# A spectral filter and a gated convolution on one core: forward part by 32 channels, back half in time order, a list that knows PSUM and transfers

## The chip, the cores and the metric

The kernel runs on 1 core of one Trainium2 chip. The metric is device microseconds of one launch. The kernel before was run three times: 344.11, 345.82 and 351.01 us, median 345.82.

The engines are named as in the profile: PE (TensorE, with its weight loads as PEld), DVE (VectorE), ACT (ScalarE), POOL (GpSimd) and SP (SyncE). SP only issues transfers here, and POOL mostly.

## The reference

The input x has 8 images (batch) of 3200 points by 256 channels. Every channel is filtered in the frequency domain over the 3200 points; the result goes through a gated unit with a causal convolution of five taps.

```
X = rfft(x, axis=1)                         # 1601 frequencies
y = irfft(X * (filt_r + 1j*filt_i), n=3200) # y: (8, 3200, 256)

gate = sigmoid(sum_k conv_w[k] * y_padded[:, k:k+3200, :])   # k = 0..4, four zeros ahead
val  = y @ w_val                                             # 256 x 256
out  = (gate * val) @ w_out                                  # 256 x 256, float32
```

## The kernel before, in words

The 3200 points are 100 x 32: point n = 32a + r. The transform is done in two steps of matmuls, and so is its inverse; between the two steps of the inverse the data goes through a scratch tensor in HBM (`escr`).

Per image, in the order of the data:

- `load_x`: eight loads on POOL's queue, each four values of r, all a and all channels, cast to bf16 (tile `xt`, ten buffers).
- `s1` (L417): first transform, two matmuls of 512 columns per load. `so` copies its PSUM to `so` on ACT or DVE, in an interleaved layout of four channels. `turn` (L436): four transposes of 32x32 blocks on DVE, which take pairs of bf16 as float32.
- `s2` (L446): second transform, seven units of two (the last of one) frequency groups. `xs` copies it to bf16, `zed` (L464) multiplies with the real filter (`za`) and, in a second instruction, with the imaginary one (`zb`), both on DVE.
- `inva` (L477): first step of the inverse. `ue` copies, `wr` (L498) writes the unit to `escr` through SP's queue.
- `lv` (L508, L509): eight reads of four values of r, two transfers each, only after all seven writes. `ib` (L518): second step of the inverse, `ye` (L528, ACT) copies it to `yt`, ordered by r, then a. `halo` (L535, L537) copies the last four r, shifted by one a, ahead of the first on POOL.
- Eight blocks of four r by 100 a: `conv` (L545) with diagonal weights, `gate` (L554, sigmoid on ACT), `val` (L563), `gv` (L573, the gate product on DVE), `outp` (L583), `oe` (copy `o<-ps`), `store` (L597, L598, two transfers on SP's queue).

L408 is the copy on ACT and L410 the copy on DVE, both called from `so`, `xs`, `ue`, `oe` and the tables. All PSUM tiles are of one kind, 128 x 1024 float32 with four buffers. The first 20 us also make the tables of the transforms (`cf_t`, `w_t`, `a_t`, `b_t`, `ci_t`) and load the filters (`fr_t`, `fi_t`), whose upper half of rows is a copy made by SP (L253, "doubling").

The order on every engine is written by `Plan`: a list of tasks, each with an engine and a cost in us, a rank, what it depends on, which buffers it takes and gives back, and a time until its transfer has landed (`land`). It is played once at build time: at each moment the ready task with the lowest rank gets the free engine. The resulting order is fixed; on the chip each engine runs its own in order and waits for what is not there. Transfers are only a delay in this list, and PSUM only a count of four:

```
add(f"wr{b},{u}", {"SP": 0.45}, r + 1, ..., lambda e, b=b, u=u: wr(b, u), take=..., land=3.0)
add(f"lv{b},{i}", {"SP": 0.8}, r - 2, [f"wd{b},{u}" for u in range(len(UCH))], ..., land=3.0, give=())
add("fl0", {"none": 0.0}, -100, [], None, land=26.0)
add("fl1", {"none": 0.0}, -100, [], None, land=34.0)
```

## Time and profile before

| what | value |
|---|---|
| median of three runs | 345.82 us (344.11 to 351.01) |
| profiled execution, first to last instruction | 344.8 us |
| busy: PE, ACT, DVE, POOL | 288.3, 267.8, 256.4, 68.0 us |
| mean granted TensorE clock | 0.970 |
| moved by DMA | 70.91 MB, mean 206 GB/s |
| first transform of image 0 starts | 6.0 us |
| first convolution starts | 79.1 us |
| last matmul of `outp` starts | 338.6 us |

The span is one execution; the median is of other executions of the same kernel and lies 1.0 us above it. Busy time is the time in which at least one instruction of the engine ran. A group's line in the profile gives its line in the code, the engine, the operation, what it writes and reads, the count, the busy time, the mean in ns of one, and the idle time of the engine ahead of it with what ended it.

### The profile page before, as it was taken

The numbers are of one execution on the slowest core, as the hardware profiler recorded it, in microseconds if no ns is written. First come the engines' busy times: TensorE is split into PE (matmuls) and PEld (weight loads), VectorE is DVE, ScalarE is ACT, GpSimd is POOL, SyncE is SP. The second block draws the span as 40 slices with busy tenths as digits, with TensorE's granted clock in tenths as the row PEclk, the third lists the DMA queues.
The fourth block names the chain that finished last, engine by engine and source line by source line (L and its number), as shares of the span: only waits on it lengthen the run. The fifth ranks groups of instructions, "written<-read, shape, count | busy, mean of one in ns | idle before, by whom it ended". The sixth has DMA issues, their size and how long they took to land.

```text
span 344.8 us, 9785 instructions
## 1 busy us (share of the span) xinstructions
PE 288.3 (84%) x3988; PEld 191.6 (56%) x3988; DVE 256.4 (74%) x340; ACT 267.8 (78%) x309; POOL 68.0 (20%) x142
## 2 busy tenths in 40 slices
PE   2634677639999987999779997999999999999992
PEld 0023031326667755776457764776577677766762
DVE  4985477938698996889849994989798999734541
ACT  3954286928898987898849986998999789887663
POOL 8687455210112112110211011100100000001000
PEclk9999999969999999899989998999999999999997
DMA  6999999995899989898869969795677568778544
GB/s 95 155 168 163 213 192 195 206 238 168 199 232 247 272 233 231 245 229 251 170 200 207 271 176 250 214 245 171 199 208 221 156 204 261 234 214 248 160 144 143
DMA packets 57421, 70.91 MB, mean 206 GB/s; under 512 B 8608, under 2 KB 37152, under 8 KB 57376
## 3 DMA queue, kind: packets, MB, share of 16 engines
q1 hardware_dynamic: 45344, 55.20, 53.4%
q0 software_dynamic: 12032, 15.08, 29.0%
q8 instruction: 31, 0.51, 0.6%
q14 instruction: 14, 0.11, 0.1%
HBM read 43.78 MB, written 39.85 MB: 243 GB/s over the span
## 4 chain that ended last, share of the span: by engine, by line
PE 43%; DMA 24%; DVE 15%; ACT 7%; issue 4%; POOL 4%; SPq 1%; ACTq 0%; POOLq 0%; DVEq 0%
DMA vt<-escr 13%; PE ps L583 12%; PE ps L545 10%; DMA xt<-in_x_dram 6%; PE ps L563 6%; DVE tt L436 5%; DVE gv L573 5%; PE ps L417 5%; PE ps L518 5%; PE ps L477 4%; DMA fi_t<-in_filt_i_dram 3%; PE ps L446 3%; ACT o L408 2%; DVE xs L410 2%; POOL xt L161 2%
## 5 line engine op out<-in xcount | busy, mean ns | idle before, releaser
L573 DVE TENSOR_TENSOR gv<-ps,gt 128x800 bf16<-128x800 f32 x64 | 62.7, 980 | 19.9 <-PE ps L563 13.6
L408 ACT ACTIVATE o<-ps 100x1024 f32<-100x1024 f32 x59 | 61.0, 1035 | 16.9 <-PE ps L583 12.9
L410 DVE CAST xs<-ps 128x1024 bf16<-128x1024 f32 (+1 forms) x44 | 50.4, 1145 | 29.0 <-PE ps L446 29.0
L583 PE MATMUL ps<-wo_t,gv 128*100 128x256 bf16 x512 | 68.7, 278 | 2.7 <-DVE gv L573 1.1
L545 PE MATMUL ps<-yt,dg_t 64*64 64x400 bf16 x1280 | 67.3, 339 | 0.3
L408 ACT ACTIVATE so<-ps 128x1024 bf16<-128x1024 f32 x53 | 54.5, 1029 | 15.9 <-PE ps L417 11.1
L528 ACT ACTIVATE yt<-ps 128x800 bf16<-128x800 f32 x64 | 53.9, 846 | 15.9 <-PE ps L518 15.7
L583 PEld LDWEIGHTS <-gv 128*100 128x100 bf16 x512 | 54.5, 125 | 18.6 <-DVE gv L573 9.0
L161 POOL DMA_DIRECT2D xt<-in_x_dram x64 | 35.4, 556 | 124.5 <-PE ps L417 119.8
L554 ACT ACTIVATE gt<-ps 128x800 bf16<-128x800 f32 x64 | 54.1, 847 | 6.5 <-PE ps L545 5.3
L417 PE MATMUL ps<-xt,cf_t 100*128 100x512 bf16 x128 | 47.5, 462 | 12.2 <-DMA xt<-in_x_dram 11.2
L563 PE MATMUL ps<-yt,wv_t 128*128 128x400 bf16 x256 | 54.4, 335 | 0.5 <-ACT gt L554 0.5
L408 ACT ACTIVATE u<-ps 128x1024 bf16<-128x1024 f32 (+1 forms) x46 | 44.9, 982 | 7.2 <-PE ps L477 6.6
L518 PE MATMUL ps<-ci_t,vt 104*128 104x100 f16 x512 | 34.3, 212 | 16.5 <-DMA vt<-escr 16.4
L518 PEld LDWEIGHTS <-vt 104*128 104x128 bf16 x512 | 29.6, 100 | 30.1 <-DMA vt<-escr 19.8
L545 PEld LDWEIGHTS <-dg_t 64*64 64x64 bf16 x1280 | 34.5, 108 | 17.3 <-issue 4.2
L436 DVE STREAM_TRANSPOSE tt<-so 128x1024 f32<-128x1024 f32 x32 | 40.6, 1272 | 3.2 <-ACT so L408 3.2
L464 DVE TENSOR_TENSOR za<-xs,fr_t 128x1024 bf16<-128x1024 bf16 (+1 forms) x56 | 36.1, 649 | 1.4 <-ACT xs L408 0.2
L464 DVE TENSOR_TENSOR zb<-xs,fi_t 128x1024 bf16<-128x1024 bf16 (+1 forms) x56 | 35.5, 640 | 1.4 <-DMA fi_t<-in_filt_i_dram 1.4
L477 PE MATMUL ps<-zb,b_t 64*64 64x256 bf16 x416 | 29.7, 294 | 4.4 <-DVE zb L464 4.4
L477 PE MATMUL ps<-za,a_t 64*64 64x256 bf16 x416 | 30.3, 298 | 2.4 <-DVE za L464 2.1
L446 PE MATMUL ps<-tt,w_t 64*64 64x256 bf16 x416 | 24.2, 305 | 9.0 <-DVE tt L436 4.4
(93 smaller groups left out, 181.9 us busy)
## 6 DMA issues: line engine op xcount, KB each, us to landing
out_dram<-o SPq DMA_DIRECT2D x64, 384.0 KB
xt<-in_x_dram POOLq DMA_DIRECT2D x64, 200.0 KB, 6.7
escr<-u SPq DMA_DIRECT2D x48, 256.0 KB
vt<-escr SPq DMA_DIRECT2D x64, 192.0 KB
escr<-u SPq DMA_DIRECT2D x8, 128.0 KB
vt<-escr SPq DMA_DIRECT2D x64, 16.0 KB
out_dram<-o SPq DMA_DIRECT2D x64, 16.0 KB
fr_t<-in_filt_r_dram POOLq DMA_DIRECT2D x8, 56.0 KB, 4.7
```

Source lines behind the costliest of these rows:

```text
L408: nc.scalar.activation(dst, src, AF.Copy, **kw)
L410: nc.vector.tensor_copy(dst, src)
L417: nc.tensor.matmul(ps[:, 512 * h:512 * h + 512], lhsT=cf_t[0:L].rearrange("p h c i -> p (h c i)"), rhs=xv[:, DQ // 2 * h:DQ // 2 * h + DQ ...
L436: nc.vector.transpose(dst, src)
L464: (nc.vector if e == "DVE" else nc.gpsimd).tensor_tensor(z[:, :, 0:nm * D], xs_[:, :, 0:nm * D], f[:, :, m0:m0 + nm, :].rearrange("p h m d ...
L477: nc.tensor.matmul(ps[64 * h:64 * h + 64, 512 * t + D * a:512 * t + D * a + D], lhsT=tab[rows, h, m0 + a, :], rhs=zz[w][rows, h, D * a:D * ...
L518: nc.tensor.matmul(ps[:, o:o + L], lhsT=v[0:NV, a, 128 * dh:128 * dh + 128], rhs=ci_t[0:NV, :], start=True, stop=True)
L545: nc.tensor.matmul(ps[64 * dh:64 * dh + 64, 512 * r:512 * r + RC * L], lhsT=dg_t[rows, dh, k, :], rhs=y[rows, dh, RC * j + k:RC * j + k + ...
L554: nc.scalar.activation(g[...], ps[:, :].rearrange("p (h n) -> p h n", h=2)[:, :, 0:RC * L], AF.Sigmoid)
L563: nc.tensor.matmul(ps[:, 512 * eh:512 * eh + RC * L], lhsT=wv_t[:, dh, 128 * eh:128 * eh + 128], rhs=y[:, dh, H + RC * j:H + RC * j + RC, ...
L573: nc.vector.tensor_tensor(gv_[...], ps[:, :].rearrange("p (h n) -> p h n", h=2)[:, :, 0:RC * L], g[...], op=ALU.mult)
L583: nc.tensor.matmul(ps[0:L, D * a:D * a + D], lhsT=gv_[:, eh, L * a:L * a + L], rhs=wo_t[:, eh, :], start=(eh == 0), stop=(eh == 1))
```

## The change

- **Loads.** Four loads of eight r per image instead of eight of four; six `xt` buffers instead of ten. All four are held until the last `s1` of the image.
- **Forward part by 32 channels.** `s1` makes one chunk of 32 channels over all r with four matmuls of 256 columns, so it needs the whole image of x. There are eight chunks; each is copied and then transposed by itself (eight transposes of 512 pairs), in a plain layout without interleaving.
- **Filter products.** Real and imaginary filter lie in one tile `f_t`; one DVE instruction makes both products, reading `xs` twice.
- **Inverse.** Reads and `ib` go in seven pieces of five or four r. `ye` may run on ACT or DVE and writes y in time order; the scale moves into the tables. y has two fixed tiles with four zero points ahead; the halo copies go.
- **Back half by up to 512 points in time order.** Blocks of 4, 4, 4, 4, 3, 3, 3 groups of 128 points. `conv` reads y shifted by k points and needs all of the image's y. `gv` writes its result so that `outp` has 128 output rows per matmul pair; an image has 25 such pairs of matmuls instead of 32. `store` is one transfer per block.
- **The list.** PSUM tiles are named by the list (four tags, the one that came free first); transfers are a resource `DMA` with a cost; ranks come from a table of offset and step per kind of task; costs and landing times are others.

```diff
-RC = 4
-NCH = R // RC
+NQ = 8
+CQ = 32
+NX = 4
-ICH = [NCH - 1] + list(range(NCH - 1))
+ICH = [(0, 5), (5, 5), (10, 5), (15, 5), (20, 4), (24, 4), (28, 4)]
+BLK = [(0, 4), (4, 4), (8, 4), (12, 4), (16, 3), (19, 3), (22, 3)]
...
+PAR = dict(
+    PERIOD=72.97,
+    OFF=dict(cv=156.07, ia=-128.75, ib=-197.48, lv=-31.3, lx=-117.23, op=28.61, s1=-95.0, s2=19.16, vl=14.51,
+             z=-219.82),
+    STEP=dict(cv=10.032, ia=33.214, ib=0.337, lv=2.627, lx=23.302, op=46.79, s1=0.678, s2=9.262, vl=9.77,
+             z=39.345),
+)
+NPS = 4
+def rank_of(par, s, b, k):
+    return par["PERIOD"] * b + par["OFF"][s] + par["STEP"][s] * k
...
+            slot = None
+            if "ps" in t["take"]:
+                slots.sort()
+                held[n] = slot = slots.pop(0)[1]
...
+    NXT, NSO, NXS, NZ, NU, NVB, NGB, NOB = 6, 3, 3, 3, 4, 4, 3, 4
+    y_t = [cpool.tile([128, 2, H + N], BF16, name=f"y{n}") for n in range(2)]
...
     def psum():
-        return pp.tile([128, 1024], FP32, name="ps", tag="ps")
+        return pp.tile([128, 1024], FP32, name="ps", tag=f"ps{g['slot']}")
...
+        for j in range(NX):
+            nc.tensor.matmul(ps[:, w * CQ * j:w * CQ * j + w * CQ],
                              lhsT=cf_t[0:L].rearrange("p h c i -> p (h c i)"),
-                             rhs=xv[:, DQ // 2 * h:DQ // 2 * h + DQ // 2], start=True, stop=True)
+                             rhs=st["X", b, j][0:L, :, CQ * q:CQ * q + CQ],
+                             start=True, stop=True)
...
     def turn(b, q):
         if q == 0:
-            st["T", b] = tpool.tile([128, DQ, 32, E], BF16, name="tt")
-        w = DQ // 4
-        src, dst = (t_[:, w * q:w * q + w].rearrange("p q r e -> p (q r e)").bitcast(FP32)
-                    .rearrange("p (q r w) -> p q w r", r=32, w=E // 2)
-                    for t_ in (st["SO", b], st["T", b]))
-        nc.vector.transpose(dst, src)
+            st["T", b] = tpool.tile([128, 32, D], BF16, name="tt")
+        src = st.pop(("SO", b, q))[...].rearrange("p r w -> p (r w)").bitcast(FP32)
+        dst = st["T", b][...].rearrange("p i d -> p (i d)").bitcast(FP32)
+        V.transpose(dst.rearrange("p (i k) -> p k i", i=32)[:, CQ // 2 * q:CQ // 2 * q + CQ // 2],
+                    src.rearrange("p (r k) -> p k r", r=32))
...
+    def zed(b, u):
+        V.tensor_tensor(z[:, :, :, 0:nm * D],
+                        t[:, :, 0:nm * D].unsqueeze(1).to_broadcast((128, 2, 2, nm * D)),
+                        f_t[:, :, :, m0:m0 + nm, :].rearrange("p w h m d -> p w h (m d)"),
+                        op=ALU.mult)
...
     def ye(b, i, e):
+        copy(e, y_t[b % 2][:, :, H:H + N].rearrange("p h (n r) -> p h n r", r=R)
+             [:, :, :, r0:r0 + nr],
+             ps[:, :].rearrange("p (h n) -> p h n", h=2)[:, :, 0:nr * L]
+             .rearrange("p h (r n) -> p h n r", n=L))
-    def halo(b):
...
     def gv(b, j):
+        V.tensor_tensor(
+            t[:, :, 0:nm, :].rearrange("p h a n -> p h n a"),
+            ps[:, :].rearrange("p (h n) -> p h n", h=2)[:, :, 0:128 * nm]
+            .rearrange("p h (n a) -> p h n a", a=nm),
+            gt[:, :, 0:128 * nm].rearrange("p h (n a) -> p h n a", a=nm), op=ALU.mult)
     def outp(b, j):
-        for a in range(RC):
+        for a in range(nm):
             for eh in range(2):
+                nc.tensor.matmul(ps[:, D * a:D * a + D], lhsT=t[:, eh, a, :],
+                                 rhs=wo_t[:, eh, :], start=(eh == 0), stop=(eh == 1))
     def store(b, j):
-        nc.sync.dma_start(out=dst[0:96], in_=o[0:96])
-        nc.sync.dma_start(out=dst[96:L], in_=o[96:L])
+        dst = out[b, 128 * m0:128 * m0 + 128 * nm, :].rearrange("(p a) d -> p (a d)", a=nm)
+        nc.sync.dma_start(out=dst, in_=o[:, 0:nm * D])
...
+                add(f"li{b},{j}", {"POOL": 0.6}, r, ["pool"],
+                    lambda e, b=b, j=j: load_x(b, j), take=("xt",), land=1.0)
+                add(f"lx{b},{j}", {"DMA": 2.2}, r, [f"li{b},{j}"], None, land=2.0)
...
+            add(f"t{b},{q}", {"DVE": 0.68}, r, [f"so{b},{q}"] + ([f"t{b},{q - 1}"] if q else []),
+                lambda e, b=b, q=q: turn(b, q), take=("t",) if q == 0 else (), give=("so",))
...
+            add(f"wi{b},{u}", {"SP": 0.35}, r, [f"ue{b},{u}"] + ([f"wi{b},{u - 1}"] if u else []),
+                lambda e, b=b, u=u: wr(b, u), take=("e",) if u == 0 else (), land=0.6)
+            add(f"wd{b},{u}", {"DMA": 0.44 * nm}, r, [f"wi{b},{u}"], None, give=("u",), land=2.0)
...
+            add(f"vi{b},{i}", {"SP": 0.7}, r, [f"wd{b},{u}" for u in range(len(UCH))],
+                lambda e, b=b, i=i: lv(b, i), take=("v",), land=0.6)
+            add(f"lv{b},{i}", {"DMA": 0.14 * nr}, r, [f"vi{b},{i}"], None, land=1.6)
...
+    add("pool", {"none": 0.0}, -100, [], None, land=19.0)
+    for c, t in enumerate((22.0, 27.0)):
+        add(f"fl{c}", {"none": 0.0}, -100, [], None, land=t)
```

507 lines of the change are left out of this document (245 added, 262 removed).

## The prediction

> **What bounds the kernel now.** I read the page first, then three stretches side by side, then the chain in order of time, then the groups by form, and last the first 50 us instruction by instruction. The page:
>
> ```profile
> span 344.8 us, 9785 instructions
> ...
> PE 288.3 (84%) x3988; PEld 191.6 (56%) x3988; DVE 256.4 (74%) x340; ACT 267.8 (78%) x309; POOL 68.0 (20%) x142
> ...
> DMA vt<-escr 13%; PE ps L583 12%; PE ps L545 10%; DMA xt<-in_x_dram 6%; PE ps L563 6%; DVE tt L436 5%; DVE gv L573 5%; PE ps L417 5%; PE ps L518 5%; PE ps L477 4%; DMA fi_t<-in_filt_i_dram 3%; PE ps L446 3%; ACT o L408 2%; DVE xs L410 2%; POOL xt L161 2%
> ```
>
> No engine is full over the whole span, and the chain hops between PE and three transfers. The stretches (us, then busy us of PE, PEld, DVE, ACT, POOL, then clock, DMA share, GB/s) say why:
>
> ```profile
> 60.00:80.00 20.00, 11.20 (x187) 7.03 (x189) 12.66 (x17) 12.39 (x15) 3.80 (x8) 0.83 0.97 220
> 0.00:80.00 80.00, 45.21 (x459) 19.50 (x463) 53.93 (x111) 47.10 (x54) 43.54 (x91) 0.96 0.98 181
> 80.00:300.00 220.00, 204.99 (x3052) 145.32 (x3045) 185.26 (x213) 190.85 (x223) 23.45 (x49) 0.98 0.82 219
> 300.00:344.80 44.80, 38.10 (x488) 26.77 (x484) 17.25 (x17) 29.89 (x34) 0.97 (x2) 0.96 0.62 184
> ```
>
> The first 80 us are a start-up: PE is busy for 45.2 of them, DMA is at 0.98. From 80 to 300 PE has 205 of 220, ACT 191, DVE 185: all three are close together, PE ahead. At the end PE works nearly alone. The start-up ends where the causal convolution begins:
>
> ```profile
> L545 PE MATMUL ps<-yt,dg_t x1280: 327/329/539, 79.1 to 335.5; 64*64 64x400 bf16 x183
> ```
>
> Pieces of the chain (start, us, what):
>
> ```profile
> 34.36 11.60 DMA xt<-in_x_dram
> ...
> 63.07 11.63 DMA vt<-escr
> ...
> 91.92 5.78 DMA escr<-u
> ...
> 167.33 6.89 DMA vt<-escr
> ...
> 202.51 0.88 PE ps L583 x8
> ...
> 242.86 4.60 DMA vt<-escr
> ...
> 338.99 1.02 ACT o L408
> ```
>
> So PE's last matmul ends at 338.9. From 80 to there it has 288.3 - 45.2 = 243.1 us of work in 258.9 us, 0.939. The kernel is 80 us of start-up, then a stretch that PE fills, then 344.8 - 338.9 = 5.9 us of last copy and store. The median shown, 345.82, is 1.0 above the span; I add that 1.0 at the end.
>
> **The change part by part.** The groups by form:
>
> ```profile
> L583 PE MATMUL ps<-wo_t,gv 128*100 128x256 bf16 x512 | 68.7, 278 | 2.7 <-DVE gv L573 1.1 <-ACT yt L528 0.2
> L573 DVE TENSOR_TENSOR gv<-ps,gt 128x800 bf16<-128x800 f32 x64 | 62.7, 980 | 19.9 <-PE ps L563 13.6 <-ACT gt L554 6.1
> L408 ACT ACTIVATE o<-ps 100x1024 f32<-100x1024 f32 x59 | 61.0, 1035 | 16.9 <-PE ps L583 12.9 <-ACT yt L528 1.5 <-DMA vt<-escr 1.4
> L554 ACT ACTIVATE gt<-ps 128x800 bf16<-128x800 f32 x64 | 54.1, 847 | 6.5 <-PE ps L545 5.3
> L528 ACT ACTIVATE yt<-ps 128x800 bf16<-128x800 f32 x64 | 53.9, 846 | 15.9 <-PE ps L518 15.7
> L410 DVE CAST xs<-ps 128x1024 bf16<-128x1024 f32 x38 | 46.4, 1222 | 28.8 <-PE ps L446 28.8
> L408 ACT ACTIVATE u<-ps 128x1024 bf16<-128x1024 f32 x40 | 41.4, 1040 | 5.8 <-PE ps L477 5.1 <-ACT xs L408 0.4 <-DMA vt<-escr 0.2
> L436 DVE STREAM_TRANSPOSE tt<-so 128x1024 f32<-128x1024 f32 x32 | 40.6, 1272 | 3.2 <-ACT so L408 3.2
> L161 POOL DMA_DIRECT2D xt<-in_x_dram x64 | 35.4, 556 | 124.5 <-PE ps L417 119.8 <-DMA xt<-in_x_dram 2.1 <-DMA fi_t<-in_filt_i_dram 0.9
> L464 DVE TENSOR_TENSOR za<-xs,fr_t 128x1024 bf16<-128x1024 bf16 x48 | 32.8, 689 | 1.2
> L464 DVE TENSOR_TENSOR zb<-xs,fi_t 128x1024 bf16<-128x1024 bf16 x48 | 32.5, 682 | 1.4 <-DMA fi_t<-in_filt_i_dram 1.4
> L410 DVE CAST xs<-ps 128x512 bf16<-128x512 f32 x6 | 4.0, 659 | 0.2 <-PE ps L446 0.2
> L408 ACT ACTIVATE u<-ps 128x512 bf16<-128x512 f32 x6 | 3.6, 593 | 1.5 <-PE ps L477 1.5
> L464 DVE TENSOR_TENSOR za<-xs,fr_t 128x512 bf16<-128x512 bf16 x8 | 3.2, 405 | 0.2 <-ACT xs L408 0.2
> ```
>
> *PE.* Output points go in 25 groups of 128 per image in place of 32 of 100, so 50 matmuls of L583 replace 64. Eight back to back took 0.88 us, 0.11 each: 14 x 0.11 = 1.5 us per image, 12.3 us in all. PE is the fullest engine from 80 us on, so I count all of it. Convolution, value, first transform and inverse stream the same columns in other pieces: nothing.
>
> *ACT and DVE, per image.* ACT's slope is (1040 - 593)/512 = 0.87 ns per element, so 768 cost about 0.82 us. Output copies: 8 x 1.035 becomes 4 x 1.035 + 3 x 0.82, -1.7. Gate and inverse copies have the same elements in seven instructions, -0.2 each. Gate product: 8 x 0.98 becomes 4 x 1.22 + 3 x 0.95, -0.1. Filter products: slope (689 - 405)/512 = 0.555 ns, so 2048 elements take 1.26 against 1.37 for the pair, -0.8 over the image. Transposes: eight of half the size, 0.66 each by the ratio of the casts (659 to 1222), against four of 1.27, +0.4. Sum -2.5 of 65.5 us, some 10 us per engine over the run. These engines are not the bound; it can only shorten the 258.9 - 243.1 = 15.8 us in which PE stands idle after 80. Bounds 0 and 15.8; I take 4, nearer to nothing, because the waits on vt above (4.6 to 6.9 us) are part of it and stay.
>
> *Access steps, which no row shows.* The transposes read and write at steps of 8 bytes now; after the change they read at 64 and write at 512. The gate product writes single bf16 values 256 bytes apart. The inverse copy (L528) reads PSUM 400 bytes apart and writes runs of 10 bytes. A gain has no reason. The nearest rows are the plain forms above, so I take no extra; the other end is twice the rate per element. It is priced as a rival. The Trainium skill speaks against the change here: "SBUF — State Buffer", in the note on cachelines under "Door 1: The DMA port swizzle", says that SBUF wants at least two hits per 16-byte line and that each access to a new line is penalised. No run here shows it; a step of 8 bytes keeps that rule and the new steps break it.
>
> *The product with a repeated operand.* It could lose its 0.555 ns per element and go at the 1.1 ns of the casts; I take 0.555, since its inner runs stay contiguous bf16 like the rows'. The Trainium skill ("VectorE: DVE Perf Modes", "What auto-detection actually checks") asks only for 16-bit tensors with step one, which agrees.
>
> *Queues.* On POOL 32 of 64 loads (0.556 each) and the halo copies go; POOL waits most of the time, so nothing in the middle. On SP 28 issues per image replace 39; SP waits on ACT, nothing. A load's transfer is longer, but four bring the same image. The wait added is that the first transform needs all of x and the convolution all of y: behind these PE instructions stand the other image's matmuls, which the list has put where it believes the data to be there.
>
> *Start-up.* What sets it (start, us, engine, line, what it waited for):
>
> ```profile
> 20.89 3.32 SPq L253 DMA_DIRECT2D fi_t<-fi_t  x2
> ...
> 28.28 1.29 DVE L464 TENSOR_TENSOR zb<-xs,fi_t 128x1024 bf16<-128x1024 bf16 x2 [1.40 <-DMA fi_t<-in_filt_i_dram]
> ...
> 31.50 2.63 SPq L253 DMA_DIRECT2D fi_t<-fi_t  x2
> ...
> 42.85 1.28 DVE L464 TENSOR_TENSOR za<-xs,fr_t 128x1024 bf16<-128x1024 bf16 x2
> ...
> 46.00 1.03 PE L417 MATMUL ps<-xt,cf_t 100*128 100x512 bf16 x2 [0.42 <-DMA xt<-in_x_dram]
> ```
>
> The doubling of the first filter half was issued by 24.2 and used 4.1 later; the second, issued by 34.1, is thus in at about 38. The products that need it ran only at 42.85: DVE held copies of image 1 ahead of them, whose x came till 46. The new list has transfers as a resource and ranks most of image 0's products ahead of image 1. So: filters at 37 (four fewer loads ahead on POOL, -1), four products 42, inverse and copy 43.5, write 5.8 (the escr row above) -> 49.5, read 5.8 (between 4.6 and 6.9) -> 55, seven inverse chunks and copies of about 1 us -> 62. The convolution starts at 62 in place of 80. The list itself believes in filters at 27 and an idle POOL at 19, both too early by these rows, so it will still queue things behind unlanded data; the bounds are 55 and 80.
>
> *Sum.* PE work 288.3 - 12.3 = 276.0. By 60 PE had done 45.2 - 11.2 = 34.0, by 62 say 35. Left 241, at 0.939 takes 256.7. 62 + 256.7 + 5.9 = 324.6, less 4, is 320.6; with the 1.0, **321 us**, 7% less.
>
> **The rivals.** *The strides cost (slower).* Place: gate product, transposes, inverse copies. At twice the rate: 6400 x 1.10 ns = 7.0, 4096 x 1.10 = 4.5, 6400 x 0.87 = 5.6, together 17.1 us per image on DVE and ACT. They would need (524.2/8 - 2.5 + 17.1)/2 = 40 us each per image, against 276/8 = 34.5 for PE, and become the bound. At 0.92 of their time (they now reach 0.855 together in the middle) that is 43.5, against 34.5/0.939 = 36.7 for PE in my forecast: +6.8 over seven overlapped images, 321 + 48 = 369. At two fifths of that price, 19 us, nothing measurable is left of the gain; from two thirds on it is slower than before. For it: the old layout's 8-byte steps. Against: no row shows any loss. The skill's cacheline rule would bring this outcome.
>
> *The start-up stays* (the new list stalls behind its own optimistic landings; the change does not do what it says there). Convolution at 80: 276.0 - 45.2 = 230.8, over 0.939 = 245.8; 80 + 245.8 + 5.9 - 4 + 1 = 329. For: the landings above. Against: image 1 goes first in fewer places of the list.
>
> *The product falls to the slow rate.* 2048 x 1.1 + 0.1 = 2.35 against 1.37, +6.4 us per image on DVE, from 32 to 38, some 3 us per image beyond PE: about 345.
>
> *DMA becomes the bound.* At 0.82 over 220 us it needs 180 us of the middle; my forecast, 25 us shorter with 18 of them in the start-up, leaves some 210. It would not bind, but keeps the vt waits; inside my range.
>
> **How the numbers follow.** Forecast 321 (own range 309 to 331): 0.43. Start-up stays, 325 to 340: 0.15. A part of the stride price, 334 to 354: 0.13. The whole of it, 352 to 385: 0.24. Slow product: 0.05. The range of 302 to 360 reaches into the stride rival, because it holds much of the chance, and to the lower bound of start-up and idle time. About 2% (339 to 353 as no change) is what a measurement can tell here. Faster 0.57: the forecast, most of the second, a bit of the third; same 0.17; slower 0.26.
>
> **What would show it.** First convolution near 62; L583 at 400 matmuls and near 54 us busy; transposes near 0.66, gate products near 1.22 and 0.95, inverse copies near 1.02 us; the product near 1.26. If transposes, gate products and inverse copies show 1.4 times these, the strides decide and I am wrong. If the first convolution stands at 75 or later, the start-up step is wrong. If PE is busy under 0.9 after its start, the order in the queues is.

## The result, and the profile after

The changed kernel takes **516.07 us** (median; 514.44 to 519.21) against 345.44 for the kernel before on the same chip: **1.495 times as long, interval 1.485 to 1.505**. I had forecast 321, with a range of 302 to 360. The slower side stood there only as a rival (the strides cost, 369 us), and that was far too small as well.

The page of the changed kernel: span, then busy time and share of each engine.

```profile
span 512.7 us, 9126 instructions
...
PE 324.1 (63%) x3786; PEld 193.9 (38%) x3812; DVE 454.6 (89%) x326; ACT 250.3 (49%) x268; POOL 41.0 (8%) x88
```

Before, PE led with 84% and DVE had 74%. Now DVE has 454.6 us of work against 256.4, and PE is at 63%. In stretches (us, then busy us of PE, PEld, DVE, ACT, POOL, then clock, DMA share, GB/s), cut at the first convolution:

```profile
0.00:85.20 85.20, 39.99 (x510) 27.78 (x511) 62.70 (x111) 44.23 (x50) 31.12 (x70) 0.74 0.84 167
85.20:300.00 214.80, 146.08 (x1669) 84.35 (x1684) 202.74 (x123) 113.46 (x120) 9.83 (x18) 0.84 0.53 146
```

From 85 to 300 DVE is busy for 202.7 of 214.8 us (0.94) and PE for 146.1 (0.68): before it was PE that had 0.93. DVE is the bound of the whole steady part. Which of its instructions, the groups by form say (busy us, mean ns of one, then idle time and what ended it):

```profile
L589 DVE TENSOR_TENSOR gv<-ps,gt 128x1024 bf16<-128x1024 f32 x32 | 150.2, 4741 | 14.7 <-PE ps L578 10.1 <-ACT gt L569 1.8 <-ACT y L189 1.6
L589 DVE TENSOR_TENSOR gv<-ps,gt 128x768 bf16<-128x768 f32 x24 | 85.6, 3615 | 4.7 <-PE ps L578 3.3 <-issue 1.0 <-ACT u L189 0.2
L460 DVE STREAM_TRANSPOSE tt<-so 128x512 f32<-128x512 f32 x64 | 70.7, 1110 | 8.4 <-ACT so L189 8.3
L601 PE MATMUL ps<-wo_t,gv 128*128 128x256 bf16 x400 | 65.7, 317 | 74.6 <-DVE gv L589 74.5
L487 DVE TENSOR_TENSOR z<-xs,f_t 128x2048 bf16<-128x2048 bf16 x48 | 60.2, 1268 | 4.9 <-DMA wv_t<-in_moe_w_val_dram 4.8
...
L189 ACT ACTIVATE y<-ps 128x1000 bf16<-128x1000 f32 x19 | 23.9, 1272 | 12.5 <-PE ps L540 12.4
```

The gate product takes 235.8 us in 56 instructions; before it was 62.7 in 64. That is 173 us of DVE's extra 198. The transposes add 30 (70.7 against 40.6). PE's last product (L601) waits 74.5 us for the gate product, where before it waited 1.1. The start-up did not shorten either; the first of the convolution's matmuls (L559) starts at 85.2 us, before at 79.1:

```profile
L559 PE MATMUL ps<-y,dg_t x1120: 319/375/632, 85.2 to 496.6; 64*64 64x512 bf16 x107, 64*64 64x384 bf16 x80
```

### The profile page after: what moved, and what is told of

Its sections match the earlier page's. It is cut to its first block, busy times and chain, and to the rows that moved or that the text cites. A ratio compares the mean times of both kernels' runs of the same rounds, so it can differ in the third digit from the quotient of the medians.

```text
span 512.7 us, 9126 instructions
## 1 busy us (share of the span) xinstructions
PE 324.1 (63%) x3786; PEld 193.9 (38%) x3812; DVE 454.6 (89%) x326; ACT 250.3 (49%) x268; POOL 41.0 (8%) x88
## 5 line engine op out<-in xcount | busy, mean ns | idle before, releaser
L589 DVE TENSOR_TENSOR gv<-ps,gt 128x1024 bf16<-128x1024 f32 (+1 forms) x56 | 235.1, 4258 | 19.3 <-PE ps L578 13.5
L601 PE MATMUL ps<-wo_t,gv 128*128 128x256 bf16 x400 | 65.7, 317 | 74.6 <-DVE gv L589 74.5
L559 PE MATMUL ps<-y,dg_t 64*64 64x512 bf16 (+1 forms) x1120 | 78.5, 415 | 10.5 <-DVE gv L589 8.5
L460 DVE STREAM_TRANSPOSE tt<-so 128x512 f32<-128x512 f32 x64 | 70.7, 1110 | 8.4 <-ACT so L189 8.3
L601 PEld LDWEIGHTS <-gv 128*128 128x128 bf16 x400 | 41.0, 111 | 95.7 <-DVE gv L589 80.3
L569 ACT ACTIVATE gt<-ps 128x1024 bf16<-128x1024 f32 (+1 forms) x56 | 52.3, 933 | 43.6 <-PE ps L559 42.9
L487 DVE TENSOR_TENSOR z<-xs,f_t 128x2048 bf16<-128x2048 bf16 (+1 forms) x56 | 66.6, 1202 | 4.9 <-DMA wv_t<-in_moe_w_val_dram 4.8
L444 PE MATMUL ps<-xt,cf_t 100*128 100x256 bf16 x256 | 49.1, 329 | 29.3 <-DMA xt<-in_x_dram 25.0
L578 PE MATMUL ps<-y,wv_t 128*128 128x512 bf16 (+1 forms) x198 | 60.9, 409 | 5.9 <-DVE gv L589 3.2
L559 PEld LDWEIGHTS <-dg_t 64*64 64x64 bf16 x1120 | 35.8, 122 | 38.9 <-issue 23.5
L189 ACT ACTIVATE xs<-ps 128x1024 bf16<-128x1024 f32 (+1 forms) x39 | 37.3, 968 | 25.0 <-PE ps L471 25.0
```

The costliest lines, as they stand in the source:

```text
L189: nc.scalar.activation(dst, src, AF.Copy, **kw)
L444: nc.tensor.matmul(ps[:, w * CQ * j:w * CQ * j + w * CQ], lhsT=cf_t[0:L].rearrange("p h c i -> p (h c i)"), rhs=st["X", b, j][0:L, :, CQ * ...
L460: V.transpose(dst.rearrange("p (i k) -> p k i", i=32)[:, CQ // 2 * q:CQ // 2 * q + CQ // 2], src.rearrange("p (r k) -> p k r", r=32))
L487: V.tensor_tensor(z[:, :, :, 0:nm * D], t[:, :, 0:nm * D].unsqueeze(1).to_broadcast((128, 2, 2, nm * D)), f_t[:, :, :, m0:m0 + nm, :].rear ...
L559: nc.tensor.matmul(ps[64 * dh:64 * dh + 64, 512 * r:512 * r + 128 * nm], lhsT=dg_t[rows, dh, k, :], rhs=y[rows, dh, 128 * m0 + k:128 * m0 ...
L569: nc.scalar.activation(t[:, :, 0:n], ps[:, :].rearrange("p (h n) -> p h n", h=2)[:, :, 0:n], AF.Sigmoid)
```

## The experiments

Line numbers are those of each run's own kernel; they move by a few. Ratios are to the kernel before on the same chip. e1 to e4 and e8 were run once each, so they have no interval; beside e1 to e4 the kernel before took 349.0 us, beside e8 346.6.

### Is it the writes or the reads of the gate product, and which property of the writes?

Three edits of the changed kernel and one kernel for the prices alone. **e1_gv_read** keeps the order of `gv` in memory, but the instruction walks along the writes and takes the steps on its inputs (16 bytes in PSUM, 8 in `gt`):

```diff
-            t[:, :, 0:nm, :].rearrange("p h a n -> p h n a"),
+            t[:, :, 0:nm, :],
             ps[:, :].rearrange("p (h n) -> p h n", h=2)[:, :, 0:128 * nm]
-            .rearrange("p h (n a) -> p h n a", a=nm),
-            gt[:, :, 0:128 * nm].rearrange("p h (n a) -> p h n a", a=nm), op=ALU.mult)
+            .rearrange("p h (n a) -> p h a n", a=nm),
+            gt[:, :, 0:128 * nm].rearrange("p h (n a) -> p h a n", a=nm), op=ALU.mult)
```

> The gate product walks its result in storage order and takes both inputs at a step (16 and 8 bytes) instead. If the cost of 4.74 us lies in the writes (my theory), the product falls to 1.2 to 1.4 us, DVE's busy time from 455 to about 285 us and the run to some 350 us (335 to 370): the first convolution stays near 85 us and the transposes stay at 1.1 us, so it does not get below the kernel before. If the cost lies in the permuted walk as such, whichever side is stepped, the product stays above 3 us and the run above 450 us.

**e2_gv_pad** leaves the walk and puts the rows of `gv` 272 bytes apart in place of 256:

```diff
-        t = st["GV", b, j] = gpool.tile([128, 2, 4, 128], BF16, name="gv")
+        t = st["GV", b, j] = gpool.tile([128, 2, 4, 136], BF16, name="gv")
...
```

> Same walk as the changed kernel, but the four rows of the result lie 272 bytes apart instead of 256. If writes to a power-of-two step collide with each other (rival), the product falls to 2.5 us or less and the run below 420 us. If every write to a new place pays, whatever the step (my theory), nothing changes: product 4.7 us, run 505 to 525 us.

**e3_gv_weights** writes the product plainly in time order, and the last product's weight load takes every fourth (third) column:

```diff
...
-                nc.tensor.matmul(ps[:, D * a:D * a + D], lhsT=t[:, eh, a, :],
+                nc.tensor.matmul(ps[:, D * a:D * a + D], lhsT=t[:, eh, 0:128 * nm].rearrange("p (n a) -> p n a", a=nm)[:, :, a],
```

> The product is written plainly in time order; the weight load of the output matmuls takes every fourth (third) column instead. If only DVE pays for steps, the product is 1.2 us, weight loads stay near 98 ns and the run is that of the stepped read, some 350 us. If the weight load pays as well, it rises to 200 ns or more, the group of eight output matmuls from about 0.9 to 1.7 us, and the run is 20 us or more above the stepped read.

**e4_micro** leaves the computation out and runs the disputed operations alone, four times each. Here every k-th element of the tile is written:

```
for k, nm in ((1, "wb"), (2, "wd"), (4, "wh"), (8, "wp"), (16, "wq")):
    t = pool.tile([128, 2, 128, 4, k], BF16, name=nm)
    prod(t[:, :, :, :, 0], pvc, gtc)
```

> Leaves the whole computation out (the output is filled with zeros) and repeats single forms four times each. Product of 1024 elements, written 2, 4, 8, 16 and 32 bytes apart (wb, wd, wh, wp, wq), then as in the changed kernel (wgate), with 272 bytes (wpad) and with float32 results (wfour); and with stepped reads (rboth, rpsum, rgate). Theory of new lines: 1.2 us up to 8 bytes, a jump from 16 on, wgate and wpad alike at 4.7; reads at most 1.4. Rival of colliding steps: wp and wq near 1.2 to 2.4 and wpad near them, wgate alone at 4.7. Transposes: tplain and teight 0.66, and of tread and twrite one carries the 0.45 us that tboth shows over it; by the theory of writes it is twrite. Copies of y: ywrite carries the loss if writes pay, yread if it is PSUM.

Measured: e1 359.4 us, e2 514.9, e3 358.2. The groups of e1, e2 and e3 in turn:

```profile
L589 DVE TENSOR_TENSOR gv<-ps,gt 128x1024 bf16<-128x1024 f32 x32 | 38.8, 1213 | 11.6 <-PE ps L578 5.8 <-ACT gt L569 4.8 <-issue 0.9
```

```profile
L589 DVE TENSOR_TENSOR gv<-ps,gt 128x1024 bf16<-128x1024 f32 x32 | 146.6, 4627 | 14.4 <-PE ps L578 7.9 <-ACT y L189 2.4 <-ACT so L189 2.3
```

```profile
L600 PEld LDWEIGHTS <-gv 128*128 128x128 bf16 x400 | 41.1, 112 | 13.4 <-DVE gv L589 6.2 <-issue 3.8
L589 DVE TENSOR_TENSOR gv<-ps,gt 128x1024 bf16<-128x1024 f32 x32 | 38.9, 1214 | 10.8 <-PE ps L578 5.5 <-ACT gt L569 4.8 <-issue 0.5
```

The same numbers, the same memory order, only the walk turned: 4741 ns becomes 1213, which is the 1.22 that the prediction wanted of the plain form, and the run falls by 157 us. It is not a collision of rows a power of two apart, since 272 bytes cost 4627. And the turn is free where PE takes it: a weight load with a step of 8 bytes takes 112 ns, against 99 in e1 with plain rows, and loads lie beside matmuls. The prices alone, in e4 (written tile, mean ns; `wb` to `wq` have steps of 2, 4, 8, 16 and 32 bytes, `wgate` is the changed kernel's product, `wfour` the same in float32, `rboth` writes plainly and takes both inputs at a step, 16 bytes in PSUM and 8 in `gt`, `agate` is a copy on ACT with the writes of `wgate`; of the transposes `tplain` has no steps, `tread` reads at 64 bytes, `twrite` writes at 512, `tboth` does both):

```profile
L61 ACT ACTIVATE agate<-pa 128x1024 bf16<-128x1024 f32 x4 | 19.0, 4738 | 0.1
L56 DVE TENSOR_TENSOR wgate<-pv,gt 128x1024 bf16<-128x1024 f32 x4 | 18.9, 4725 | 0.0
L56 DVE TENSOR_TENSOR wp<-pv,gt 128x1024 bf16<-128x1024 f32 x4 | 18.8, 4694 | 0.0
...
L56 DVE TENSOR_TENSOR wq<-pv,gt 128x1024 bf16<-128x1024 f32 x4 | 17.8, 4450 | 0.0
L56 DVE TENSOR_TENSOR wh<-pv,gt 128x1024 bf16<-128x1024 f32 x4 | 9.6, 2412 | 0.0
L56 DVE TENSOR_TENSOR wfour<-pv,gt 128x1024 f32<-128x1024 f32 x4 | 7.7, 1914 | 0.0
L56 DVE TENSOR_TENSOR wd<-pv,gt 128x1024 bf16<-128x1024 f32 x4 | 5.1, 1264 | 0.0
...
L56 DVE TENSOR_TENSOR rboth<-pv,gt 128x1024 bf16<-128x1024 f32 x4 | 4.9, 1216 | 0.1
L120 DVE STREAM_TRANSPOSE twrite<-sb 128x512 f32<-128x512 f32 x4 | 4.8, 1210 | 0.0
...
L56 DVE TENSOR_TENSOR wb<-pv,gt 128x1024 bf16<-128x1024 f32 x4 | 4.7, 1167 | 0.0
L120 DVE STREAM_TRANSPOSE tboth<-sq 128x512 f32<-128x512 f32 x4 | 4.6, 1148 | 0.0
L115 DVE STREAM_TRANSPOSE tread<-sq 128x512 f32<-128x512 f32 x4 | 4.3, 1064 | 0.0
...
L115 DVE STREAM_TRANSPOSE tplain<-sb 128x512 f32<-128x512 f32 x4 | 2.7, 686 | 0.0
```

What the product pays for is where it writes. The price of a bf16 value rises from 1.14 ns (step 2 bytes) to 1.23 (4), 2.36 (8) and 4.6 (16), and then stays (4.35 at 32, 4.6 at 256). That 8 bytes already double it was not expected. Steps in the inputs, PSUM included, cost the product next to nothing (1216 against 1167 ns); ACT pays the same as DVE. The transposes are different: they pay for reads at 64 bytes (1064) and for writes at 512 (1210), against 686, and both together cost no more (1148); I had put it on the writes alone. Of the inverse copy's steps e4 shows almost no price: with the same reads and the same runs of 10 bytes 64 apart it takes 1047 ns on ACT and 1200 on DVE, plain 1002 and 1196.

### Is that one walk enough by itself?

**e8_before_step** makes the kernel before walk point by point through its own gate product, so that successive writes lie 200 bytes apart; nothing else is touched.

```diff
+        def walk(t):
+            return t.rearrange("p h (a n) -> p h n a", a=RC)
...
-            gv_[...], ps[:, :].rearrange("p (h n) -> p h n", h=2)[:, :, 0:RC * L], g[...],
+            walk(gv_[...]), walk(ps[:, :].rearrange("p (h n) -> p h n", h=2)[:, :, 0:RC * L]),
+            walk(g[...]), op=ALU.mult)
```

> The kernel before with one part alone: its gate product walks point by point, so that neighbouring writes lie 200 bytes apart; inputs are read in the same order. Theory of new lines: 4.5 ns per element, product 3.6 to 3.8 us against 0.98, 64 x 2.7 = 173 us more on DVE, run 480 to 530 us. If the loss needs the other parts of the change, the run stays below 420 us.

546.4 us, above what was expected. Its group:

```profile
L576 DVE TENSOR_TENSOR gv<-ps,gt 128x800 bf16<-128x800 f32 x64 | 246.2, 3884 | 41.0 <-PE ps L563 30.4 <-ACT gt L554 8.1 <-issue 1.4
```

980 ns became 3884, and the old kernel lost 200 us by this line alone. Taken out of the one kernel the walk saves 157 us, put into the other it costs 200: the main cause is shown from both sides.

### What is left when the writes are mended

e3, at 358.2 us, is still above the kernel before (349.0 beside it, one run each). **e5_both** adds the old interleaved layout of four channels around the transposes (read by the first product's moving side, and undone by the second's):

```diff
-                             rhs=st["X", b, j][0:L, :, CQ * q:CQ * q + CQ],
+                             rhs=st["X", b, j][0:L, :, CQ * q:CQ * q + CQ]
+                             .rearrange("p r (c e) -> p c r e", e=4),
...
-                                 lhsT=w_t[rows, i, :], rhs=t_[rows, i, :],
+                                 lhsT=w_t[rows, i, :], rhs=t_[rows, :, i, :],
...
```

> The changed kernel with the plain gate product of e3 and with the interleaved layout of four channels back around the transposes (their steps are 8 bytes again). My theory: transposes 0.70 us, 64 x 0.38 = 24 us off DVE, which then has some 262 us; the start-up is not touched, first convolution at 80 to 86; the run at 335 to 350 us, level with the kernel before within 3%. Rival, that DVE alone held the run of e3 back: the gain shows in full and the run is under 335.

**e6_start** is e5 with a list that is told later landings at the start, as e3's trace has them, and **e7_list** besides that takes a newly searched set of ranks, longer scratch landings and seven buffers for the reads:

```diff
-    add("pool", {"none": 0.0}, -100, [], None, land=19.0)
+    add("pool", {"none": 0.0}, -100, [], None, land=28.5)
+    add("early", {"DMA": 33.0}, -1000, [], None)
...
-    for c, t in enumerate((22.0, 27.0)):
+    for c, t in enumerate((31.0, 40.5)):
```

> As e5, and the list is told when data lands at the start by e3's trace: POOL free at 28.5 us, both filter halves at 31 and 40.5, x of image 0 at 14, other transfers not before 33. Ranks and all else as they are. If the late start comes from a list that believes in early landings, the first convolution comes 8 to 15 us earlier (near 72) and the run is 5 to 15 us shorter than e5. Rival, that transfers set it whatever the order: first convolution within 3 us of e5, run within 2%.

> As e6, and the list is also told longer landings of the scratch tensor (3.5 us after a write, 3.2 after a read) and 0.115 us per pair of matmuls in the second inverse step, has seven buffers for its reads instead of four, and other ranks, searched for these costs. If the waits for vt in e3 (28 us on the weight loads) come from the list's short landings and the four buffers, they fall below 12 us and the run to 318 to 332 us, 4 to 8% under the kernel before. If they are DMA time as such, they stay above 20 us and the run within 2% of e6.

e5: 354.2 us, **1.022 [1.014, 1.029]**. e6: 357.2, 1.030 [1.022, 1.038]. e7: 360.5, 1.041 [1.033, 1.048]. e5 is above the 335 to 350 us that I expected of it. Its transposes take 702 ns in place of 1083, 24 us less of DVE, but the time is only some 4 us below that of e3 (on another chip): DVE no longer binds. What does (e5's chain by line, then its waits, and those of the kernel before):

```profile
by line: DMA vt<-escr 18.9%; PE ps L562 12.8%; PE ps L581 9.9%; PE ps L603 8.1%; DMA escr<-u 6.4%; DMA xt<-in_x_dram 5.0%; PE ps L503 5.0%; PE ps L444 5.0%; PE ps L543 4.8%; DMA wv_t<-in_moe_w_val_dram 3.1%; issue 2.5%; PE ps L474 2.1%; DMA
...
89.30 10.53 DMA escr<-u
...
182.18 10.00 DMA vt<-escr
```

```profile
PEld L543 <- DMA vt<-escr: 28.4, 20, 4.0
PE ps L444 <- DMA xt<-in_x_dram: 27.6, 8, 6.8
...
PE ps L543 <- DMA vt<-escr: 23.5, 19, 3.8
...
PE ps L503 <- DVE z L490: 4.5, 3, 2.0
```

```profile
PE ps L518 <- DMA vt<-escr: 16.4, 6, 7.3
PE ps L417 <- DMA xt<-in_x_dram: 11.2, 8, 6.0
...
PEld L518 <- DMA vt<-escr: 19.8, 8, 7.5
```

DMA holds 36% of the chain by the page, against 24% before, and a write and a read of the scratch array take 10 us there after the first convolution, where on the chain of the kernel before they took 4.6 to 6.9. PE waits 27.6 us for x and 23.5 for vt, before 11.2 and 16.4. The list as I mended it is not the remedy: told later landings it is no faster (e6 can't be told from e5 by the intervals), searched anew it is slower (e7), the vt waits on the weight loads are 34.9 and 31.5 us, and the first convolution moves only from 83.5 to 82.2 and 78.1. That is the rival's answer in both expectations.

### One part at a time on the kernel before

**e9_one_product** takes the single filter product alone, **e10_back_half** the mended back half alone, **e11_back_product** both.

```diff
-        z = zpool.tile([128, 2, 2 * D], BF16, name="za" if which == 0 else "zb")
+        z = st["Z", b, u] = zpool.tile([128, 2, 2, 2 * D], BF16, name="z")
+        V.tensor_tensor(z[:, :, :, 0:nm * D],
+                        t[:, :, 0:nm * D].unsqueeze(1).to_broadcast((128, 2, 2, nm * D)),
+                        f_t[:, :, :, m0:m0 + nm, :].rearrange("p w h m d -> p w h (m d)"),
...
```

> The kernel before with one part of the change alone: both filters in one tile, both products in one instruction with the spectrum repeated, one z buffer in place of za and zb. VectorE's products fall from 71.6 us to about 66 (48 of 1.26 us and 8 of 0.67). Theory: VectorE does not bound the kernel before, so the time moves by 0 to 3 us down, 342 to 346. Rival: the first half product was ready 0.7 us earlier before, and the inverse step that starts on it now waits for the whole; then 346 to 352.

```diff
-ICH = [NCH - 1] + list(range(NCH - 1))
+ICH = [(0, 5), (5, 5), (10, 5), (15, 5), (20, 4), (24, 4), (28, 4)]
+BLK = [(0, 4), (4, 4), (8, 4), (12, 4), (16, 3), (19, 3), (22, 3)]
...
```

> The kernel before with the back half of the change alone (blocks of 512 points in time order, seven reads of the scratch array, stores of 512 KB), its gate product written plainly and the steps put into the weights of the last product; forward part, filter products, PSUM ring and the old way of making the list stay. TensorE's work falls by 12 us to about 276. Theory (the extra waits for the scratch array come with the forward part by chunks of channels, whose four loads of an image go out together): the waits of the inverse step for the vt tiles stay near the 20 and 16 us of before, and the time is 330 to 340. Rival (they come with the back half, where no convolution can start before all seven reads have landed): the vt waits are 26 us or more on the weight loads, and the time is 345 to 358.

> The two parts before together: the repaired back half and the single filter product on the forward part, the PSUM ring and the list of the kernel before. By the first theory 328 to 339, faster than both kernels; by the rival 343 to 358. TensorE 276 us, VectorE 10 us below that of the run with the back half alone or less.

e9, e10 and e11 take 347.7 us (1.011 [1.005, 1.017]), 352.4 (1.019 [1.011, 1.027]) and 357.5 (1.030 [1.021, 1.039]). The single product takes 1.22 us, and the products' rows fall from 71.6 us to 63.3, more than the 66 expected; none of it reaches the end. The time is in the rival's range, but 1% is within the 2% that I count as no change; that the half product ready 0.7 us earlier costs something was not shown. In e10 neither answer held: the vt waits stay near those of before, as the theory said, and the time is the rival's (its waits):

```profile
ACT gt L551 <- PE ps L541: 28.6, 31, 2.4
...
PEld L522 <- DMA vt<-escr: 18.1, 11, 8.2
```

PE's page total is 286.2 us there, only 2.1 below before, though its last product has 400 matmuls in place of 512. ACT's sigmoid waits 28.6 us for the convolution, where before it waited 5.3. Whether transfers or the old list (its ranks and costs were made for other blocks) are behind that, e18 below bears on. e11 is in the rival's range; the 10 us that DVE and the 12 us that PE should have lost there don't show in their totals (270.9 us, in e10 270.5; 284.8, before 288.3).

### The loads of x

**e12_x_once** is e5 without the loads of images 1 to 7, **e13_before_x_once** the kernel before without them, **e18_back_x_once** e10 without them.

```diff
     def load_x(b, j):
+        if b:
+            st["X", b, j] = st["X", 0, j]
+            return
...
```

> The repaired changed kernel (plain gate product, turned layout as before) without the loads of images 1 to 7: every image reads the tiles of image 0, so that part of the input is left out of what is computed; the list and all other instructions stay. Theory (the four loads of an image, issued together, hold up the scratch array's writes and reads): the vt waits fall from 28.4 and 23.5 us to below 20 and 16, and the time by 15 us or more, to 340 or less. Rival (the scratch round trip is late by itself): the vt waits stay at 25 us or more on the weight loads, and the time falls only by what the forward product waited for its loads after image 0, at most 10 us, to 344 to 352.

> The kernel before without the loads of images 1 to 7 (every image reads image 0's tiles, so that part of the input is left out of what is computed). Theory (transfers bind both kernels alike, and the change only uncovers it): it falls by as much as the repaired changed kernel did, 35 us or more, to 310 or less, and stays level with or ahead of that kernel's 312. Rival (the loads hurt the change more, by their bursts of four): it falls by 10 to 25 us only, to 321 to 336, and the 12 us of TensorE's work show as a lead of the repaired kernel.

> The kernel before with the repaired back half alone, and without the loads of images 1 to 7 (image 0's tiles are read again, so that part of the input is left out of what is computed). Without these loads the kernel before takes 320.3 us and the repaired changed kernel 312.3. Theory (the back half carries the 8 us of gain, and the transfers hid it in the run with the back half alone): 309 to 315. Rival (the gain belongs to the forward part, or the back half costs as much by its order as it saves): 318 to 326.

e12 312.3 us (0.901 [0.894, 0.908]), e13 320.3 (0.930 [0.923, 0.936]), e18 334.9 (0.968 [0.958, 0.978]). The stretches of e12, cut at its first convolution:

```profile
0.00:68.50 68.50, 37.65 (x512) 26.84 (x515) 56.23 (x111) 43.29 (x49) 25.80 (x60) 0.80 0.73 148
68.50:300.00 231.50, 225.68 (x3257) 144.23 (x3260) 206.06 (x213) 197.45 (x215) 0.00 (x0) 1.00 0.61 203
```

and of e5 and e13:

```profile
83.50:300.00 216.50, 192.88 (x2728) 121.21 (x2754) 182.90 (x190) 173.69 (x189) 9.86 (x18) 0.96 0.73 212
```

```profile
66.30:280.00 213.70, 206.25 (x3130) 148.08 (x3128) 188.28 (x218) 195.43 (x228) 7.04 (x18) 1.00 0.69 203
```

Without the loads PE is full after its start in both (225.7 of 231.5 and 206.3 of 213.7 us), and the mended change is **8 us faster** than the kernel before (the two ratios, 0.901 and 0.930, have intervals that do not meet), where PE's term had promised 12. With the loads PE of e5 has only 192.9 of 216.5. The theory held for e12: the vt waits fall from 28.4 and 23.5 to 4.2 and 2.3 us, and the time by far more than 15. The loads cost the kernel before 25 us: 13 up to the first convolution (79.1 to 66.3) and 12 behind it. They cost the mended change 42: 15 up to there (83.5 to 68.5), 24 behind it (267.1 to 243.0 us of span); the last 3 are between the profiled runs and the medians. The expectations name as a cause the four loads of an image that go out together; leaving all loads out does not part that from their bytes. Neither expectation for e13 held fully: the fall of 25 is the rival's upper bound. e18 missed both: the back half alone, on the old list and four shared PSUM buffers, is 15 us slower than the old back half even without the loads, so the 8 us are those of the whole change with its own list; the back half on the old list does not bring them.

### Can the loads be put elsewhere?

**e14_x_eight** is e5 with eight tiles for x in place of six; the three others have them too. **e15_x_held** was meant to hold image 1's loads back on GpSimd until image 0's spectra are copied; the list then put the loads of images 2 and 3 ahead of them, and eight went out at once. **e16_x_order** ties the loads of image b to the last scratch read of image b-2, in the order of the images, with image 1 free; **e17_x_order1** holds image 1 as well.

```diff
-    NXT, NSO, NXS, NZ, NU, NVB, NGB, NOB = 6, 3, 3, 3, 4, 4, 3, 4
+    NXT, NSO, NXS, NZ, NU, NVB, NGB, NOB = 8, 3, 3, 3, 4, 4, 3, 4
... (e16 and e17)
+    def hold(t):
+        nc.gpsimd.tensor_copy(held[...], t)
```

> The repaired changed kernel with eight tiles for x instead of six, so that the four loads of the next image need not wait for the last product of this one. Theory (bursts behind the last forward product collide with the scratch array's round trip): the product's waits for x fall from 27.6 us to 15 or less and the vt waits from 28.4 to 22 or less; 338 to 347. Rival (the bytes, not their moment): waits move between the two, their sum stays within 10 us of 56, and the time is 350 to 362, more at the start since all four loads of image 1 now go out there.

> As the run before it, but the loads of image 1 are held back on GpSimd until the last spectrum of image 0 is copied out (a copy of one element). Theory (the start-up is late because the loads of image 1 share the transfers with the filters and the scratch array of image 0): the first convolution starts at 65 to 72 us instead of 83.5. What it brings in the end: TensorE then has nothing of image 1 to fill the start with, so the time is 335 to 350 if the steady part keeps its pace. Rival (the start is late for the filters and the order): first convolution at 79 us or later, time 350 to 365.

> The repaired changed kernel with eight x tiles, and the loads of every image from the third on held (by a copy of one element on GpSimd) until the last scratch read of the image two before has landed. Theory (the extra cost is loads that meet the scratch round trip): the vt waits fall from 28.4 and 23.5 us to below 20 and 16, no write or read of the scratch array on the chain is longer than 7 us after 100 us, and the time is 335 to 348. Rival (the loads' bytes and their turn, not the meeting): the forward product waits longer for x, 35 us or more against 27.6, and the time is 352 to 370.

> As the run before it, and the loads of image 1 held until the last spectrum of image 0 is copied out, now with all loads in the order of the images. Theory (the start is late because image 1's loads share the transfers with filters and the scratch array of image 0): the last spectrum is copied by 46 us and the first convolution starts at 62 to 72 us. The time is then 340 to 360, since TensorE has no forward work of image 1 to lay beside it. Rival (the start is late for another reason): first convolution at 79 us or later, and 360 to 375.

e14 357.9 us (1.035 [1.025, 1.046]), e15 354.9 (1.033 [1.024, 1.041]), e16 351.0 (1.016 [1.004, 1.028]), e17 364.2 (1.051 [1.042, 1.060]). Eight tiles alone bring nothing, as the rival said: the product waits for x as long as in e5 (27.7 us; the vt waits on the weight loads fall to 18.6). e15 doesn't test what it was made for; its first convolution starts at 83.3 us, and its chain shows a meeting at its worst:

```profile
34.64 23.04 DMA escr<-u
```

A scratch write stands on the chain for 23 us beside eight loads of x. e16 shows the other side, in its waits and its chain:

```profile
PE ps L445 <- DMA xt<-in_x_dram: 24.1, 11, 7.0
...
PE ps L504 <- DVE z L491: 10.1, 7, 6.1
...
PEld L547 <- DMA vt<-escr: 7.8, 9, 2.3
```

```profile
by line: DMA xt<-in_x_dram 22.9%; PE ps L566 11.0%; PE ps L585 8.1%; PE ps L607 7.7%; DMA escr<-u 6.3%; DMA vt<-escr 5.6%; PE ps L445 5.4%; issue 4.7%; PE ps L504 3.1%; ACT y L190 2.9%; POOL xt L221 2.3%; PE ps L547 2.1%; DVE so L192 1.7%; 
...
68.42 10.22 DMA escr<-u
...
101.80 13.30 DMA xt<-in_x_dram
```

The vt waits fall from 28.4 to 7.8 us, as the theory had it, and the first convolution of e16 starts at 71.6 in place of 83.5. On the chain the loads are now the late ones: their 5.0% became 22.9%, and a scratch write of 11.8 us still stands there at 215.6. The time comes down from 354.2 to 351.0, and by the intervals that is not a sure gain; it lies between the two ranges expected. PE's own waits read differently from the chain: for x they did not grow (27.6 to 24.1 us), and for both transfers together they fell by 21.5, but those for DVE rose from 10.2 to 23.8 (the filter products' from 4.5 to 10.1, as shown) and those for ACT from 5.3 to 11.0. So what PE won on the transfers it lost waiting for the engines between them. That loads and scratch round trip trade with one another is how the chain reads; it was not shown by itself. Holding image 1 as well (e17) leaves the first convolution where it was, at 71.4, and costs 13 us at the end: the start was as the theory expected, the time as the rival did. How the 17 us that the loads cost the change more than the kernel before come about stays open; one candidate is that an image's first product needs all four of its loads at once. An order that frees both was not found. None of the kernels that compute the whole beats the kernel before.

## Why the prediction was wrong, point by point

**The access steps: the step that failed.** I priced them at nothing, with twice the rate as the other end. Measured, per image: gate product 29.5 us (235.8/8) where the plain form has 7.7 (e5: 61.8/8); transposes 8.8 against 5.6 (44.8/8); the inverse copies 1272 (ACT) and 1374 ns (DVE) for 1000 elements against 1002 and 1196 for the plain forms of e4, with 800 elements on ACT at their plain price (840 ns, before 846). So transposes and inverse copies were inside my two ends (1.6 and 1.1 to 1.3 times), and the gate product, at 3.8 to 3.9 times, was not. By the sign that I had set, 1.4 times, transposes and gate products show the loss and the inverse copies (1.25 to 1.35 times the 1.02 us) do not; and since e4 does not reproduce their loss with the same steps (1047 and 1200 ns), what they pay for stays open.

The rival named the mechanism and the place, but it had two steps wrong itself. It priced the gate product's extra at 7.0 us per image where it is 21.8 (29.5 - 7.7). And it shared the work of DVE and ACT out evenly between them: with 21.8 its sum would be (65.5 - 2.5 + 31.9)/2 = 47.5 us per image, over 0.92 51.6, and 321 + 7 x 14.9 = 425 us, not 516. But gate product and transposes are tasks of DVE alone, so DVE has 454.6 us of work and ACT 250.3. DVE's 391.9 us after the first convolution, in 427.5 us to the end (0.917), are what sets the time.

The end that I chose for the price came from the nearest rows, and none of these had single bf16 values written at a step: the old transposes' steps of 8 bytes are of float32.

The Trainium skill ("SBUF — State Buffer", the note on cachelines under "Door 1: The DMA port swizzle") had the right direction, and I gave it too little weight. The traces agree that a write which finds only one bf16 value in 16 bytes is dear (4694 ns against 1167), and disagree that two hits are free: 8 bytes apart cost 2412 ns.

**PE's twelve microseconds: there, and worth nothing with the loads in.** The last product has 400 matmuls and 53.3 us busy (e5; 54 said). PE's whole work is 276.6 us in e5, where the sum said 276.0, and without the loads 268.5 against 279.3 (e12, e13). That the first pair agrees to 0.6 is luck in part: e10 has the same 400 matmuls and 286.2, while the busy times of PE's groups, which overlap, add up to nearly the same in both (336.5 and 338.1): the total also goes by how densely the matmuls follow one another. What failed is the conclusion that all of it counts because PE is the fullest engine. In the changed kernel DVE binds, PE waits 74.5 us for the gate product alone, and the clock granted to it falls to 0.833 on average, from 0.970: its busy time is 324.1 us there. In e5 it is the transfers that it waits for, and only without the loads do 8 us of the 12 show.

**Product with a repeated operand: right.** 1268 ns in the changed kernel, 1211 in e5; 1.26 said. The Trainium skill's conditions ("VectorE: DVE Perf Modes", "What auto-detection actually checks"), 16-bit tensors with step one, were enough here, as these rows show.

**Output and gate copies: right.** 1024 and 1025 ns for 1024 elements; the sum used 1.035.

**Two slips of arithmetic**, without weight here: a transpose of half the size is 0.69 us by the ratio of the casts, not 0.66 (e5 has 0.70), and the sum ends at 321.6.

**Start-up: wrong step.** First convolution at 85.2, in the mended kernel at 83.5; 62 was said, and "75 or later" was the sign against me. I had laid the blame on DVE's order and taken the transfers' times from rows of the old trace. e6 shows that the list's beliefs about landings are worth some 1 us of it, and e7 that a new order with them is worth 5. The loads are worth most of it (e5's timeline: start, time to issue, queue):

```profile
41.45 2.24 POOL L220 DMA_DIRECT2D xt<-in_x_dram  x4 [0.82 <-DMA wo_t<-in_moe_w_out_dram]
...
52.55 5.93 SPq L523 DMA_DIRECT2D escr<-u  x4
...
57.86 2.19 POOL L220 DMA_DIRECT2D xt<-in_x_dram  x4 [14.17 <-PE ps L444]
...
58.70 0.34 SPq L533 DMA_DIRECT2D vt<-escr  x1
```

Eight loads of later images go out beside image 0's scratch writes and reads. Without the loads the convolution starts at 68.5 (e12), and with those from image 2 on held until these reads have landed at 71.6 (e16). Held loads of image 1 bring no more (e17, 71.4); they then go out at 45.2, beside the reads. I had counted the loads that go ahead on POOL, and not those that go beside. The other 6 to 10 us above 62 are not explained.

**DMA as the bound: wrongly set aside.** "It would not bind" rested on 180 us of transfers fitting into 210. The sum was not the point: in e5 DMA is at 0.73 of the middle and still holds 36% of the chain. A likely reason, not shown by itself, is that four loads of an image must all be there before its first product, and seven reads before its first convolution. The row that should have warned me was my own: the vt waits of 4.6 to 6.9 us in a kernel with DMA at 0.82.

**"PE busy under 0.9 after its start, then the order in the queues is wrong":** 0.68 in the changed kernel, where it was DVE; 0.89 in e5, where it was the transfers, and the orders that were tried did not mend it.

## What to carry to other kernels

Look at what each engine instruction writes before counting instructions: let DVE and ACT write contiguous values, and put a transposed order on an operand that is read: on an input of the product it cost 1216 against 1167 ns here, on a weight load of PE 112 against 99, and the two kernels (e1 and e3) took 359.4 and 358.2 us. An estimate for an access form that no row shows needs its far end from the form itself, so measure it alone first; the end "twice the rate" was a guess, and the kernel hung on it. A sum over two engines holds only if the work can go to either. Work saved on the fullest engine is time only if what feeds it comes in time: compare with a run in which the loads are left out.

## What the runs showed of the hardware

- A bf16 value written by DVE from PSUM costs 1.14 ns at a step of 2 bytes, 1.23 at 4, 2.36 at 8, and 4.35 to 4.6 from 16 to 272 bytes; a float32 value at 512 bytes costs 1.87 ns (1914/1024). ACT has the same price for the same writes (4738 ns for 1024, plain 1025).
- Steps of 8 and 16 bytes in the product's inputs, SBUF and PSUM, cost next to nothing (1216 to 1221 against 1167 ns). The transposes pay on either side (1064 for reads at 64 bytes, 1210 for writes at 512, 1148 for both, 686 plain).
- A weight load whose columns are 8 bytes apart takes 112 ns, 99 plain; moving operands in runs of 8 bytes show no loss (first and second product 302 and 308 ns in e5, 300 and 310 with plain runs in e3).
- The granted clock, e4 aside, was lowest where PE is busy least: 0.833 to 0.846 at 63 and 64% of the span (the changed kernel, e2, e8), 0.879 to 0.963 at 77 to 83%, 0.970 at 84% (before), and 0.950 and 0.982 at 86 and 87% (e12, e13). That is no rule: e4, with four matmuls in all, shows 1.000, and the runs of e10 alone go from 0.926 to 0.975. Whether idle time makes the low clock or the other way round was not tried.
